# Two more second products in seven blocks instead of eight, with the weight work that feeds them moved

## The chip, the cores and the metric

The kernel runs on 1 core of a Trainium2 chip. The metric is device time in microseconds (us) of one execution, the median of several; lower is better. One core has TensorE (PE, matrix products), VectorE (DVE), ScalarE (ACT), GpSimd (POOL) and SyncE (SP, here the queue of nearly all DMAs).

## The reference

Linear attention with an RMS norm, then a dense network with SiLU, then four experts with ReLU, whose outputs are added under normalised weights. All inputs are float32.

```
kv = einsum('bhsd,bhse->bhde', k, v); out = einsum('bhsd,bhde->bhse', q, kv)
x = out / sqrt(mean(out*out, -1) + 1e-6) * g_norm        # -> 2304 tokens x 512
h = x @ w_in; x = (h * sigmoid(h)) @ w_out               # 512 -> 2048 -> 512
p = probs / (probs.sum(-1) + 1e-9)
out = sum over e of p[:, e] * (relu(x @ w1[e]) @ w2[e])   # 4 experts, 512 -> 1024 -> 512
```

## The kernel before, in words

The tokens are cut in three groups of 768 (NP = 3). The dense network is cut in four experts of 512 hidden units (groups 0 to 3), the four real experts in eight halves of 512 (groups 4 to 11). A *step* n works one expert on one token group: steps -12 to -1 are the dense network (group g has steps 3g-12 to 3g-10), steps 0 to 23 the experts. So steps -6 to -4 are group 2, steps -3 to -1 group 3, steps 0 to 2 group 4.

A step has two matrix products, 512x512 by 512x768. A float32 operand is kept as a high part (ACT, `hi`) and a remainder (DVE or POOL, `lo`), and three part products are added. A product is done either in eight blocks of 12 matmuls (`second`, "plain") or by a scheme with seven block products and extra sums (`again`, "seven blocks"). The seven need the weights' four quarters' sums s1 to s4 (`fsum`, `sumw`, DVE), sums t1 to t4 of the hidden values (`sumh`, DVE), their splits (`hhi` on ACT, `hlo` on DVE, for t3 and t4 on POOL), and seven additions into the accumulator (`gather`, DVE) where plain needs four. The first product (`first`) has seven blocks in every step from -9 on. Which steps have a second product of seven blocks, the function `seven` says (L138): in before -9, -8, -7, -5, -4, -3 and all from 1 on.

TensorE's order is written by hand. Time is counted in *slots*; a block of 12 matmuls is one slot. `start[n]` is the slot at which step n begins, and a first block of step n alternates with a second block of step n-1. A step's stretch is 7 slots plus 7 or 8 for the second product of the step before it. Every other operation is put at a slot (`put(slot, f, ...)`); events are sorted by slot and recorded in that order, so the tables of slots (SUM_AT, SPLIT_AT, W1_AT, W2_AT, CONVERT) fix each engine's queue. Each engine works its queue in order and waits where an operand or a buffer isn't ready. A table's slots count from the start of the group's first step.

The names used later: L467 `gather` (acc<-ps_ox, ps_oz or ps_o), L414 `add` (f<-ps_z), L454 `sumh` (f<-f), L152 `lo` (hid, w, x), L149 `hi`, L234 `fsum`, L292 `sumw`, L196, L197 and L201 the conversion of one dense weight chunk on VectorE (`cv3` is two instructions, `cv4` one), L207 its end on POOL, L326 `xsum`, L273 and L280 the loads of an expert's first and second weights, L347 and L359 the stores and loads of split tokens. PSUM holds two banks for the second products; a bank can be written again when its `gather` has read it. Buffers: five `w2`, two `w2b` (s3, s4), seven `w1`, eight `raw`. `swap` (slot -23.6) gives the memory of the dense weights to the `raw` loads.

## Time and profile before

| what | us |
|---|---|
| three timed runs | 1147.37, 1146.85, 1147.36 (median 1147.36) |
| the profiled execution, its own time | 1146.34 |
| its span, first to last instruction | 1144.6 |
| TensorE busy | 1134.5 (99%) |
| VectorE busy | 950.2 (83%) |
| ScalarE busy | 515.7 (45%) |
| GpSimd busy | 335.1 (29%) |

The 1.7 us between span and time lie around the program. Matmuls are pipelined, so one of 12 shows 0.34 us though a block takes 2.09. All the rows quoted are of this one execution.

### The profile page before, as it was taken

The numbers are of one execution on the slowest core, as the hardware profiler recorded it, in microseconds if no ns is written. First come the engines' busy times: TensorE is split into PE (matmuls) and PEld (weight loads), VectorE is DVE, ScalarE is ACT, GpSimd is POOL, SyncE is SP. The second block draws the span as 40 slices with busy tenths as digits, with TensorE's granted clock in tenths as the row PEclk, the third lists the DMA queues.
The fourth block names the chain that finished last, engine by engine and source line by source line (L and its number), as shares of the span: only waits on it lengthen the run. The fifth ranks groups of instructions, "written<-read, shape, count | busy, mean of one in ns | idle before, by whom it ended". The sixth has DMA issues, their size and how long they took to land.

```text
span 1144.6 us, 17104 instructions
## 1 busy us (share of the span) xinstructions
PE 1134.5 (99%) x6673; PEld 1128.5 (99%) x6673; DVE 950.2 (83%) x1080; ACT 515.7 (45%) x730; POOL 335.1 (29%) x198
## 2 busy tenths in 40 slices
PE   9999999999999999999999999999999999999998
PEld 8999999999999999999999999999999999999998
DVE  3997768987987587699799899899889889889874
ACT  4885565555554454544333333333333333333334
POOL 4943213331221344132232222232232232223211
PEclk9999999999999999999999999999999999999999
DMA  9967876666656662695675776675686685686604
GB/s 365 361 241 259 296 294 245 219 208 222 229 191 212 196 235 100 249 311 196 237 240 205 234 253 203 217 253 202 216 268 208 204 271 198 205 278 207 207 32 162
DMA packets 70035, 261.23 MB, mean 228 GB/s; under 512 B 7804, under 2 KB 26180, under 8 KB 69444
## 3 DMA queue, kind: packets, MB, share of 16 engines
q1 hardware_dynamic: 69668, 260.11, 65.2%
q8 instruction: 53, 0.87, 0.3%
q14 instruction: 26, 0.21, 0.1%
q10 hardware_dynamic: 288, 0.04, 0.0%
HBM read 222.34 MB, written 37.79 MB: 227 GB/s over the span
## 4 chain that ended last, share of the span: by engine, by line
PE 88%; DVE 6%; DMA 2%; ACT 2%; issue 1%; POOL 0%; SPq 0%; DVEq 0%; ACTq 0%; POOLq 0%
PE ps_x L369 22%; PE ps_ox L369 19%; PE ps_z L369 16%; PE ps_oz L369 15%; PE ps_o L498 9%; PE ps_h L397 4%; DMA kv_raw<-in_kv 2%; DVE hid L152 1%; ACT hid L149 1%; PE p_o L858 1%; PE ps_kv L836 1%; DVE acc L467 1%; DVE f L454 1%; DVE f L414 1%; ACT f L424 1%; DMA wd_raw<-in_wd 1%
## 5 line engine op out<-in xcount | busy, mean ns | idle before, releaser
L149 ACT ACTIVATE hid<-f 128x768 fp32r<-128x768 f32 x231 | 192.1, 843 | 370.4 <-DVE f L454 195.4
L152 POOL TENSOR_TENSOR hid<-f,hid 128x768 fp32r<-128x768 f32 x82 | 162.9, 1987 | 569.9 <-ACT hid L149 438.4
L369 PE MATMUL ps_x<-x,w 128*128 128x384 f32 x1584 | 297.0, 335 | 0.0
L369 PEld LDWEIGHTS ps_x<-x,w 128*128 128x128 f32 x1584 | 277.7, 188 | 0.0
L369 PE MATMUL ps_ox<-hid,w 128*128 128x384 f32 x1392 | 261.4, 335 | 0.6 <-DVE acc L467 0.6
L369 PEld LDWEIGHTS ps_ox<-hid,w 128*128 128x128 f32 x1392 | 243.2, 188 | 1.0 <-ACT hid L149 0.9
L369 PE MATMUL ps_z<-x,w 128*128 128x384 f32 x1188 | 222.8, 335 | 0.0
L369 PEld LDWEIGHTS ps_z<-x,w 128*128 128x128 f32 x1188 | 208.3, 188 | 0.0
L369 PE MATMUL ps_oz<-hid,w 128*128 128x384 f32 x1044 | 196.4, 335 | 1.8 <-DVE acc L467 1.3
L152 DVE TENSOR_TENSOR hid<-f,hid 128x768 fp32r<-128x768 f32 x149 | 153.0, 1028 | 52.3 <-ACT hid L149 52.2
L369 PEld LDWEIGHTS ps_oz<-hid,w 128*128 128x128 f32 x1044 | 182.3, 188 | 3.0 <-DVE acc L467 2.0
L498 PE MATMUL ps_o<-hid,w 128*128 128x384 f32 x672 | 124.2, 334 | 0.0
L454 DVE TENSOR_TENSOR f<-f 128x768 f32<-128x768 f32 x116 | 115.2, 993 | 2.7 <-ACT f L424 1.2
L498 PEld LDWEIGHTS ps_o<-hid,w 128*128 128x128 f32 x672 | 117.3, 188 | 0.0
L467 DVE TENSOR_TENSOR acc<-ps_ox,acc 128x768 f32<-128x768 f32 x109 | 103.6, 951 | 14.1 <-PE ps_ox L369 13.2
L414 DVE TENSOR_TENSOR f<-ps_z,f 128x768 f32<-128x768 f32 x66 | 62.9, 953 | 39.8 <-PE ps_z L369 39.8
L449 DVE SCALAR_TENSOR_TENSOR f<-f,pb 128x768 f32<-128x768 f32 x72 | 86.6, 1203 | 2.5
L467 DVE TENSOR_TENSOR acc<-ps_oz,acc 128x768 f32<-128x768 f32 x85 | 80.8, 951 | 8.9 <-PE ps_oz L369 8.1
L149 ACT ACTIVATE w<-s 128x512 fp32r<-128x512 f32 x88 | 54.9, 624 | 54.9 <-DVE s L292 29.2
L207 POOL TENSOR_TENSOR full<-full,wd_raw 128x512 int32<-128x512 int32 x32 | 47.9, 1497 | 103.8 <-DVE full L201 60.9
L409 ACT ACTIVATE f<-ps_x 128x768 f32<-128x768 f32 x66 | 53.3, 807 | 35.1 <-PE ps_x L369 35.0
L152 DVE TENSOR_TENSOR w<-s,w 128x512 fp32r<-128x512 f32 x74 | 53.3, 727 | 5.4 <-ACT w L149 4.7
(77 smaller groups left out, 955.8 us busy)
## 6 DMA issues: line engine op xcount, KB each, us to landing
x<-x_dram SPq DMA_DIRECT2D x210, 768.0 KB, 4.3
x_dram<-x SPq DMA_DIRECT2D x42, 768.0 KB, 5.2
wd_raw<-in_wd SPq DMA_DIRECT2D x32, 512.0 KB, 4.7
raw<-in_w SPq DMA_DIRECT2D x128, 128.0 KB, 4.6
kv_raw<-in_kv SPq DMA_DIRECT2D x18, 512.0 KB, 10.3
pb<-p_dram SPq DMA_DIRECT2D x24, 384.0 KB, 5.0
q_raw<-in_qt SPq DMA_DIRECT2D x4, 1152.0 KB, 11.6
out<-o SPq DMA_DIRECT2D x6, 512.0 KB, 2.8
```

Source lines behind the costliest of these rows:

```text
L149: self.nc.scalar.activation(t[:, 0], f, AF.Copy)
L152: (eng or self.nc.vector).tensor_tensor(t[:, 1], f, t[:, 0].bitcast(F32), op=ALU.subtract)
L207: self.nc.gpsimd.tensor_tensor(f, f, self.words(c, i, 0, I32), op=ALU.add)
L369: self.nc.tensor.matmul(p[:, f, :HN], w[0][:, a, c : c + 128], x[:, b, kp, :], start=self.FRESH[k] and a == b == kp == 0, stop=b == kp == ...
L397: self.nc.tensor.matmul(p, w[:, u, c : c + 128], self.x[n, f"b{k + 1}{j + 1}"][:, v, kp, :], start=u == v == k == kp == 0, stop=v == k == ...
L409: self.nc.scalar.activation(t, self.of_ps(n, c), AF.Copy)
L414: self.nc.vector.tensor_tensor(t, self.of_ps(n, c), t, op=ALU.add)
L424: self.nc.scalar.activation(self.f[n, name], src, AF.Silu)
L449: self.nc.vector.scalar_tensor_tensor(f, src, 0.0, self.probs(n, int(name[2]) - 1), op0=ALU.max, op1=ALU.mult)
L454: self.nc.vector.tensor_tensor(f, self.f[n, a], self.f[n, b], op=ALU.subtract)
L467: self.nc.vector.tensor_tensor(a, self.of_ps(n, k), a, op=ALU.add)
L498: self.nc.tensor.matmul(self.ps[n, b][:, e, :HN], w[:, u, c : c + 128], h[:, v, kp, :], start=self.count[key] == 1, stop=self.count[key] = ...
```

## The change

Steps -6 and 0 become steps of seven blocks. Their s weights (group 2 and group 4) must then be ready for their first step, so tables of slots change: the first weights of the dense groups (`SUM1_AT`, `SPLIT1_AT`, now tables for each group), the second weights of group 2 (`SUM_AT[2]`, `SPLIT_AT[2]`), the conversions (`CONVERT`), and group 4's loads, sums and splits (the first entries of `W1_AT`, `W2_AT`). Six splits of group 4's weights and two of the tokens (b21 of steps 1 and 2) go from GpSimd to VectorE. The later places of c11, c21 and t4, which steps 0 to 22 had, now hold for the dense steps too. Each of the groups 2 and 4 splits one quarter fewer, a21.

```
-        return n >= 1 or n in (-9, -8, -7, -5, -4, -3)
+        return n >= 0 or n in (-9, -8, -7, -6, -5, -4, -3)
...
-        2: dict(a11=2.4, a12=4.4, a21=6.4, a22=14.5, s1=15.9, s4=17.1, s3=18.3, s2=29.2),
+        2: dict(a11=6.5, s1=8, s2=8.6, s4=15.5, s3=19.2, a12=20.4, a22=21.5),
...
-    CONVERT = {1: (6.5, 9, 18.5, 20.5, 22.5, 25.5, 31, 35), 2: (6, 8.5, 15, 19.2, 20.8, 22.4, 24, 31.8)}
+    CONVERT = {1: (13, 16, 18.2, 22.4, 24, 27, 30.4, 32.4), 2: (13, 16, 18.2, 22.4, 24, 27, 30.4, 32.4)}
...
-                    for name, at in (("s1", -6.6), ("s2", -6.5), ("s3", -1.6), ("s4", -1.5)):
+                    split = dict(zip(self.A, self.SPLIT1_AT[e]))
+                    sums = dict(zip(("s1", "s2", "s4", "s3"), self.SUM1_AT[e]))
+                    for name, at in sums.items():
                         put(b0 + at, self.fsum, e, 0, name)
...
-        late = 0 <= n < self.steps - 1
+        late = n < self.steps - 1
...
-        load=(-8, -4), s1=(5.5, 7.2), s2=(5.6, 7.5), s4=(9.4, 9.4), s3=(11, 9.6),
+        load=(-23.5, -4), s1=(-19, 7.2), s2=(-18.9, 7.5), s4=(-18.2, 9.4), s3=(-16.2, 9.6),
...
-        on_pool = (self.A if i == 0 else ("a12", "s3", "a22")), (("a11", "a21", "a22") if i == 0 else ())
+        on_pool = ("a12", "s3", "a22"), ()
...
-                    put(b0 + at[k] + 0.01, self.xlo, n, name, pool if k in ((0, 1, 5) if n else (1, 3, 5)) else None)
+                    put(b0 + at[k] + 0.01, self.xlo, n, name, pool if k in ((0, 5) if n else (1, 3, 5)) else None)
```

VectorE's queue in the stretch where step -7's second product alternates with step -6's first (228 to 260 us in the trace), from one `gather` of bank oz to the next; before:

```order
L467 TENSOR_TENSOR acc<-ps_oz,acc 128x2x384
L152 TENSOR_TENSOR hid<-f,hid 128x768
L414 TENSOR_TENSOR f<-ps_z,f 128x768
L454 TENSOR_TENSOR f<-f 128x768
L152 TENSOR_TENSOR w_2438<-full_1960,w_2438 128x512
L467 TENSOR_TENSOR acc<-ps_ox,acc 128x2x384
L152 TENSOR_TENSOR hid<-f,hid 128x768
L196 TENSOR_SCALAR full_2475<-full_2475 128x512
L197 TENSOR_SCALAR full_2475<-full_2475 128x512
L201 SCALAR_TENSOR_TENSOR full_2475<-wd_raw,full_2475 128x512
L152 TENSOR_TENSOR w_2480<-full_1960,w_2480 128x512
L467 TENSOR_TENSOR acc<-ps_oz,acc 128x2x384
```

and with the change (the lines from L234 on stand six further down there):

```order
L473 TENSOR_TENSOR acc<-ps_oz,acc 128x2x384
L420 TENSOR_TENSOR f<-ps_z,f 128x768
L473 TENSOR_TENSOR acc<-ps_ox,acc 128x2x384
L152 TENSOR_TENSOR hid<-f,hid 128x768
L460 TENSOR_TENSOR f<-f 128x768
L152 TENSOR_TENSOR hid<-f,hid 128x768
L152 TENSOR_TENSOR w_2455<-s,w_2455 128x512
L152 TENSOR_TENSOR w_2463<-full_1976,w_2463 128x512
L473 TENSOR_TENSOR acc<-ps_oz,acc 128x2x384
```

The conversion (L196 to L201) is gone from here, and the bank's ox `gather` stands third instead of sixth.

VectorE's queue some 15 slots later, where step -6's second product runs, from an `add` to the next `gather` but one; before:

```order
L414 TENSOR_TENSOR f<-ps_z,f 128x768
L152 TENSOR_TENSOR w_2708<-s,w_2708 128x512
L152 TENSOR_TENSOR hid<-f,hid 128x768
L196 TENSOR_SCALAR full_2475<-full_2475 128x512
L197 TENSOR_SCALAR full_2475<-full_2475 128x512
L201 SCALAR_TENSOR_TENSOR full_2475<-wd_raw,full_2475 128x512
L467 TENSOR_TENSOR acc<-ps_o,acc 128x2x384
```

and with the change:

```order
L420 TENSOR_TENSOR f<-ps_z,f 128x768
L196 TENSOR_SCALAR full_2598<-full_2598 128x512
L197 TENSOR_SCALAR full_2598<-full_2598 128x512
L201 SCALAR_TENSOR_TENSOR full_2598<-wd_raw,full_2598 128x512
L473 TENSOR_TENSOR acc<-ps_ox,acc 128x2x384
L152 TENSOR_TENSOR hid<-f,hid 128x768
L460 TENSOR_TENSOR f<-f 128x768
L152 TENSOR_TENSOR w_2724<-s,w_2724 128x512
L152 TENSOR_TENSOR hid<-f,hid 128x768
L152 TENSOR_TENSOR w_2748<-full_1976,w_2748 128x512
L473 TENSOR_TENSOR acc<-ps_oz,acc 128x2x384
```

Two gathers stand where one stood, with a `sumh` and two more weight splits between.

SP's queue at the first loads of group 4's weights (raw1 first weights, raw2 second, x2 the split tokens that a later step reads); before:

```order
L359 DMA x2_3517<-x_dram_73 128x1536
L273 DMA raw1_3550<-in_w 128x256 x2
L273 DMA raw1_3567<-in_w 128x256 x2
L359 DMA x2_3570<-x_dram_73 128x1536
L273 DMA raw1_3572<-in_w 128x256 x2
L273 DMA raw1_3588<-in_w 128x256 x2
L359 DMA x2_3605<-x_dram_73 128x1536
```

and with the change:

```order
L365 DMA x2_3512<-x_dram_73 128x1536
L286 DMA raw2_3545<-in_w 128x256 x2
L286 DMA raw2_3561<-in_w 128x256 x2
L286 DMA raw2_3568<-in_w 128x256 x2
L365 DMA x2_3572<-x_dram_73 128x1536
L286 DMA raw2_3586<-in_w 128x256 x2
L279 DMA raw1_3590<-in_w 128x256 x2
L279 DMA raw1_3607<-in_w 128x256 x2
L365 DMA x2_3610<-x_dram_73 128x1536
L279 DMA raw1_3612<-in_w 128x256 x2
L279 DMA raw1_3628<-in_w 128x256 x2
```

The second weights' eight DMAs, which stood among the token stores after them, now come first.

## Rows read from the trace of the kernel before

**Rows 1.** The page's head: the span, then busy time, share and instructions.

```profile
span 1144.6 us, 17104 instructions
PE 1134.5 (99%) x6673; PEld 1128.5 (99%) x6673; DVE 950.2 (83%) x1080; ACT 515.7 (45%) x730; POOL 335.1 (29%) x198
```

**Rows 2.** TensorE's timeline, 227 to 297 us: start, us, block [idle, releaser].

```profile
228.23 2.25 PE L369 MATMUL ps_ox<-hid,w 128*128 128x384 f32 x12
...
251.71 2.40 PE L369 MATMUL ps_oz<-hid,w 128*128 128x384 f32 x12 [0.98 <-DVE acc L467]
...
260.20 2.25 PE L498 MATMUL ps_o<-hid,w 128*128 128x384 f32 x12
...
291.50 2.24 PE L369 MATMUL ps_ox<-hid,w 128*128 128x384 f32 x12
...
296.28 0.41 PE L369 MATMUL ps_oz<-hid,w 128*128 128x384 f32 x1 [0.45 <-ACT hid L149]
```

**Rows 3.** Stretch by stretch, one a step: length, each engine's busy time, clock, DMA.

```profile
199.01:228.23 29.22, 29.22 (x170) 29.22 (x169) 26.96 (x31) 15.60 (x22) 9.31 (x5) 1.00 0.62 214
228.23:260.20 31.97, 30.09 (x169) 29.16 (x169) 27.35 (x31) 16.98 (x25) 10.51 (x6) 1.00 0.65 223
260.20:291.50 31.30, 31.30 (x182) 31.30 (x182) 23.57 (x33) 16.09 (x25) 6.88 (x5) 1.00 0.67 235
291.50:321.43 29.93, 29.48 (x170) 29.19 (x170) 27.38 (x31) 14.91 (x22) 7.20 (x4) 1.00 0.59 205
...
442.44:473.73 31.29, 31.29 (x181) 31.29 (x181) 22.09 (x22) 14.97 (x20) 11.58 (x6) 1.00 0.59 223
473.73:503.09 29.36, 29.36 (x169) 29.18 (x169) 24.12 (x27) 14.60 (x20) 8.45 (x5) 1.00 0.76 262
```

**Rows 4.** VectorE's timeline: start, us, instruction [idle before it, releaser].

```profile
230.39 2.04 DVE L454 TENSOR_TENSOR f<-f 128x768 f32<-128x768 f32 x1
...
250.70 0.95 DVE L467 TENSOR_TENSOR acc<-ps_oz,acc 128x768 f32<-128x768 f32 x1
...
371.77 0.96 DVE L414 TENSOR_TENSOR f<-ps_x,f 128x768 f32<-128x768 f32 x1 [1.20 <-PE ps_x L369]
```

**Rows 5.** VectorE by form: xcount | busy us, mean ns of one | idle before.

```profile
L152 DVE TENSOR_TENSOR hid<-f,hid 128x768 fp32r<-128x768 f32 x149 | 153.0, 1028 | 52.3 <-ACT hid L149 52.2
L454 DVE TENSOR_TENSOR f<-f 128x768 f32<-128x768 f32 x116 | 115.2, 993 | 2.7 <-ACT f L424 1.2
L467 DVE TENSOR_TENSOR acc<-ps_ox,acc 128x768 f32<-128x768 f32 x109 | 103.6, 951 | 14.1 <-PE ps_ox L369 13.2
...
L414 DVE TENSOR_TENSOR f<-ps_z,f 128x768 f32<-128x768 f32 x66 | 62.9, 953 | 39.8 <-PE ps_z L369 39.8
L152 DVE TENSOR_TENSOR w<-s,w 128x512 fp32r<-128x512 f32 x74 | 53.3, 727 | 5.4 <-ACT w L149 4.7
L152 DVE TENSOR_TENSOR w<-raw,w 128x512 fp32r<-128x512 f32 x29 | 37.1, 1281 | 0.0
L152 DVE TENSOR_TENSOR x<-acc,x 128x768 fp32r<-128x768 f32 x33 | 33.6, 1030 | 10.9 <-ACT x L149 10.9
...
L201 DVE SCALAR_TENSOR_TENSOR full<-wd_raw,full 128x512 int32<-128x512 int32 x32 | 22.0, 689 | 0.6
L196 DVE TENSOR_SCALAR full<-full 128x512 f32<-128x512 f32 x32 | 21.1, 661 | 12.0 <-ACT full L189 11.7
...
L197 DVE TENSOR_SCALAR full<-full 128x512 int32<-128x512 int32 x32 | 14.7, 458 | 1.1
...
L234 DVE TENSOR_TENSOR s<-full 128x512 f32<-128x512 f32 x12 | 10.6, 884 | 0.0
```

**Rows 6.** SP's issues of L273, 355 to 375 us, and how long they took to land.

```profile
359.58 6.04 SPq L273 DMA_DIRECT2D raw<-in_w  x4
...
DMA to landing us min/median/max: 2.2/4.8/6.0
```

**Rows 7.** GpSimd's timeline, 228 to 232 us.

```profile
230.08 1.53 POOL L152 TENSOR_TENSOR w<-s,w 128x512 fp32r<-128x512 f32 x1 [10.46 <-ACT w L149]
```

More of the change, by code (lines that the diff above doesn't have):

```diff
@@ L219 @@
     )
-    SUM_AT = {1: (5, 5.1, 6.5, 8), 2: (15.4, 15.5, 16.8, 18), 3: (7.6, 7.7, 12, 14)}
+    SUM1_AT = {1: (-7.6, -7.5, -2.6, -2.4), 2: (-7.6, -7.5, -5.1, -4.5), 3: (-7.6, -7.5, -5.1, -4.5)}
+    SPLIT1_AT = {
[3 rows of a table added]
+    }
+    SUM_AT = {1: (5, 5.1, 6.5, 8), 2: (7.2, 7.5, 9.4, 9.6), 3: (7.6, 7.7, 12, 14)}
     SPLIT_AT = {
         1: dict(a11=6, s4=7.2, s3=8.6, s1=10.8, s2=11.8, a12=14.8, a22=16),
-        2: dict(a11=2.4, a12=4.4, a21=6.4, a22=14.5, s1=15.9, s4=17.1, s3=18.3, s2=29.2),
+        2: dict(a11=6.5, s1=8, s2=8.6, s4=15.5, s3=19.2, a12=20.4, a22=21.5),
         3: dict(a11=6, s1=8.5, s2=10.5, s4=12.5, s3=14.5, a12=16, a22=18, a21=18.2),
     }
-    CONVERT = {1: (6.5, 9, 18.5, 20.5, 22.5, 25.5, 31, 35), 2: (6, 8.5, 15, 19.2, 20.8, 22.4, 24, 31.8)}
+    CONVERT = {1: (13, 16, 18.2, 22.4, 24, 27, 30.4, 32.4), 2: (13, 16, 18.2, 22.4, 24, 27, 30.4, 32.4)}
     def fsum(self, e, i, name):
@@ L579, in first_events @@
                 if e > 0:
-                    for name, at in (("s1", -6.6), ("s2", -6.5), ("s3", -1.6), ("s4", -1.5)):
+                    split = dict(zip(self.A, self.SPLIT1_AT[e]))
+                    sums = dict(zip(("s1", "s2", "s4", "s3"), self.SUM1_AT[e]))
+                    for name, at in sums.items():
                         put(b0 + at, self.fsum, e, 0, name)
-                    for k in range(7):
-                        put(b0 - 9 + 2 * k, self.fhi, e, 0, k)
-                        put(b0 - 8.6 + 2 * k, self.flo, e, 0, k, pool if k in (1, 4, 6) else None)
-                        if self.A[k][0] == "s":
-                            put(b0 + (-1.4 if k == 2 else -8.5 + 2 * k), self.done_sum, e, 0, self.A[k])
-                    put(b0 + 3.6, self.done_full, e, 0)
+                        end = max(split[name] + 0.4, *(sums[x] for x, of in self.SUMS.items() if name in of), -99)
+                        put(b0 + end + 0.05, self.done_sum, e, 0, name)
+                    for k, at in enumerate(split.values()):
+                        put(b0 + at, self.fhi, e, 0, k)
+                        put(b0 + at + 0.4, self.flo, e, 0, k, pool if k in (1, 4, 6) else None)
+                    put(b0 + max(*split.values(), *sums.values()) + 0.5, self.done_full, e, 0)
                     for at, name in zip(self.SUM_AT[e], ("s1", "s2", "s4", "s3")):
@@ L673 @@
     W1_AT = dict(
-        load=(-23.2, -13), s1=(-11, -7.6), s2=(-10.9, -7.5), s4=(-4.9, -5.1), s3=(-6.9, -4.5),
+        load=(-21.4, -13), s1=(-11, -7.6), s2=(-10.9, -7.5), s4=(-4.9, -5.1), s3=(-6.9, -4.5),
         op=((-13.2, -11.2, -9.2, -7.2, -5.2, -3.2, -1.2), (-7.9, -7.8, -6.8, -5.8, 0.5, 6, 6.8)),
@@ L677 @@
     W2_AT = dict(
-        load=(-8, -4), s1=(5.5, 7.2), s2=(5.6, 7.5), s4=(9.4, 9.4), s3=(11, 9.6),
+        load=(-23.5, -4), s1=(-19, 7.2), s2=(-18.9, 7.5), s4=(-18.2, 9.4), s3=(-16.2, 9.6),
         op=(
-            dict(s1=6.6, s4=10.4, s3=11.5, a11=7.2, a12=8.6, a21=15.2, a22=17.7, s2=29.4),
+            dict(s1=-18.4, s4=-16.6, s3=-15.6, a11=6.6, s2=9, a12=14.6, a22=17),
             dict(a11=6.5, s1=8, s2=8.6, s4=15.5, s3=19.2, a12=20.4, a22=21.5),
@@ L738, in events @@
             put(b0 + 12.2, self.ps.pop, (n, "z"))
-            for slot, name in ((4.3, "c11"), (10.3, "c22"), (12.25, "c12"), (14.05 if n else 13.1, "c21")):
+            for slot, name in ((4.3, "c11"), (10.3, "c22"), (12.25, "c12"), (14.05, "c21")):
                 put(b0 + slot, self.relu, n, name)
@@ L743, in events @@
             put(b0 + 14.07, self.pb.pop, n)
-            if self.seven(n):
-                self.seven_events(put, n)
-            else:
-                for slot, name in ((5.3 if n else 6.15, "c11"), (10.5, "c22"), (12.5, "c12"), (14.1, "c21")):
-                    put(b0 + slot, self.hhi, n, name)
-                    put(b0 + slot + 0.01, self.hlo, n, name, pool if name == "c22" else None)
-                self.plain_events(put, n)
+            self.seven_events(put, n)
         end = self.start[self.steps]
```

3 rows, old and new, of the table SPLIT1_AT are left out of this document.

## The prediction

> **What bounds the kernel now.** The page's head comes first: TensorE is busy 1134.5 of 1144.6 us [rows 1], so whatever shortens TensorE's own row of work shortens the kernel, and everything else counts only where it makes TensorE wait. TensorE's timeline is read next: between waits the blocks follow each other without a break. The fifteen blocks from 260.20 to 291.50 [rows 2] give 31.30 / 15 = 2.087 us a block, which is one slot. Then the stretches, one a step [rows 3]. An undisturbed one of fourteen blocks lasts 29.22 us (199.01 to 228.23). The next, also of fourteen, lasts 31.97: 2.75 us of waits, the last of them at 251.71 for an `acc` of VectorE [rows 2]; that `gather` started at 250.70 and took 0.95 [rows 4], and freed the bank too late. The stretch from 291.50 has fourteen blocks and lasts 29.93: 0.71 us, around 296.28 [rows 2, 3]. These two places, 3.46 us together, lie inside the change's reach. Stretches that VectorE fills to 26.96 of 29.22 us ran without a wait [rows 3]; I take that as the nearest row for what it can carry.
>
> **TensorE's part.** Seven block products instead of eight: 12 matmuls fewer in step -6 and 12 in step 0, two blocks, 2 x 2.087 = 4.17 us. They lie on the path itself, since neither stretch (260.20 to 291.50, 442.44 to 473.73) holds a wait [rows 3]. Nothing hides them, so this gain is sure unless something else comes late.
>
> **VectorE's part.** A converted step needs 3 gathers, 4 hidden sums and 1 split more on VectorE: 3 x 0.951 + 4 x 0.993 + 1.028 = 7.85 us [rows 5], twice. Six weight splits and two token splits come from GpSimd. All of that lies beside TensorE; it costs nothing as long as VectorE isn't late. So I count each stretch anew, from the order of the changed program and the mean durations of rows 5 (a conversion is L196 + L197 + L201 = 0.661 + 0.458 + 0.689 = 1.81; a weight sum 0.884; a weight split from `s` or `full` 0.727).
>
> Common to a stretch of seven blocks in the dense part: 7 gathers 6.66, 5 hidden splits 5.14, 4 hidden sums 3.97, 3 adds 2.86, together 18.63 us. To that come
>
> - the stretch of step -7's second product (before: 228.23 to 260.20): 4 weight splits, 4 weight sums, 1 conversion, 2.91 + 3.54 + 1.81 = 8.26, so 26.89 us in 29.2. Before it was 27.35 in 31.97. The conversions and a12, a21 no longer stand between the gathers there, the light part is the front, where the three waits were.
> - that of step -6's: 4 weight splits and 5 conversions, 2.91 + 9.04 = 11.95, so 30.58 us in 29.2, where before it was 23.57 in 31.30. It is over full by 1.38.
> - that of step -5's: 3 splits, 4 sums, 2 conversions, 2.18 + 3.54 + 3.62 = 9.34, so 27.97 in 29.2.
> - that of step 0's (before: 442.44 to 473.73): the measured 22.09 [rows 3], plus 4 gathers 3.80, 2 hidden splits 2.06, 2 hidden sums 1.99, 1 token split 1.03, 2 weight splits from `raw` 2.56, less one split 0.73 and one ReLU 0.95 (priced as a gather) that now fall outside: 31.85 in 29.2, over full by 2.65. The stretch after it holds 24.12 in 29.36 and has room to catch up.
>
> **Sum of the likeliest case.** The blocks give 4.17. The 2.75 of waits go: the bank's `gather` that ended them now has three instructions fewer ahead of it and no conversion. The 0.71 goes too: TensorE waited there for a bank that a plain step's last gather had just read, and with step -6 in seven blocks no plain step stands there. At 0 to 1 that border moves to -1 to 0, where the gather comes after a stretch of light VectorE work; I count nothing. Together 7.63. Against it stand new waits in the two over full stretches. Their bounds: nothing, if VectorE's lag is carried and worked off later, and 1.38 + 2.65 = 4.03, if all of it becomes waiting. I take 1.3, a third, because a bank is written again three slots (6.3 us) after its block ended, so a gather may start 5.3 us late before TensorE waits, and a lighter stretch follows each. So 7.63 - 1.3 = 6.3 us faster. The profiled execution took 1146.34, which is 1.02 under the median of 1147.36; I take the difference off the median: 1141.0 us.
>
> **Other edits, at nothing.** ScalarE gains three high parts a converted step beside 16 of 31 us of work [rows 3]. GpSimd has four hidden splits more and nine weight and token operations less; it's at 7 to 12 of 31 us. The loads of group 4's second weights now come first in SP's queue. The first four DMAs of that place were issued from 359.58 over 6.04 us, held by the memory of the dense weights, and land in 2.2 to 6.0 us [rows 6]. The sum that reads them stands at slot -19, 371.5 us in this trace (291.50 is slot -57; 38 slots and 0.71 us of waits later), and later sums wait for later tiles. VectorE idles just then, 1.20 us before 371.77 [rows 4], and its queue is short; a landing late by a microsecond or two is covered. Behind the sum are an `add` and gathers of steps -2 and -3, and behind these TensorE. The token loads that the eight DMAs pass are read some twelve slots later by the table of slots.
>
> GpSimd and VectorE: a hidden sum at 230.39 took 2.04 us against a mean of 0.993 while GpSimd ran a split from 230.08 for 1.53 [rows 4, 5, 7], so it ran when GpSimd had ended, some 1.05 us late. The Trainium skill (SBUF — State Buffer, section Who interferes with whom) says that a VectorE instruction with two SBUF inputs and a GpSimd one that reads SBUF lock each other out for the whole instruction; the trace agrees with the 1.05 us. It speaks against the four new hidden splits on GpSimd (up to 4 x 1.05 = 4.2 us of VectorE's time) and for the nine operations taken off it (up to 9.5). My sum holds the mean of such delays in its durations and nothing more.
>
> **Rivals.**
> 1. *Clean*: VectorE carries its lag everywhere and no new wait comes. For it: the stretch with 26.96 busy had none, and 27.38 was reached in 29.93 [rows 3]. Against it: 30.58 and 31.85 are above anything in the rows. 1147.36 - 7.63 = 1139.7 us.
> 2. *All of the excess waits*: the lag turns into waits where it arises, 4.03 us. 1147.36 - 7.63 + 4.03 = 1143.8 us.
> 3. *VectorE becomes the bound, slower than before*. Its own waits for ScalarE and TensorE can't be filled: in the full stretch 29.22 - 26.96 = 2.26 us stayed idle [rows 3]. With 2.26 in each, the stretches of -6, -5 and 0 need 32.84, 30.23 and 34.11 us, over by 3.62, 1.01 and 4.89, together 9.52. If the four new GpSimd splits each hold up an instruction by 1.05 as at 230.39, 4.2 more: 13.7. 1147.36 - 7.63 + 13.7 = 1153.4 us. It decides from 9.9 us of new waits on (7.63 + 2.3). Against it: before, the same idle time was there, and VectorE shows lag without any wait in most stretches. Without the 4.2 it ends at 1149.2, no change that can be measured.
> 4. *The three waits stay*, since they come from the burst at the end of the stretch before and not from the conversions. 1141.0 + 2.75 = 1143.8, as rival 2.
>
> **Chances and range.** What a measurement of this kernel can tell from no change is about 0.2%, 2.3 us. The likeliest case (1140 to 1142.5) has 0.50, clean 0.17, rivals 2 and 4 together 0.20, between there and no change 0.08, slower 0.05. So faster 0.87, within 0.2% 0.08, slower 0.05. The range from 1139.2 (clean, less half a microsecond of scatter as the three runs show) to 1144.2 (rivals 2 and 4 with the same scatter) leaves out the last two.
>
> **What would show it.** In the changed profile, the stretches of steps -6 and 0 have fourteen blocks and last 29.2 us plus waits; if both show 31.3 the first step is wrong. No wait for `acc` between step -7's first and last block, or rival 4 holds. VectorE busy near 30 us and TensorE's new waits, if any, in step -6's and step 0's stretches, and 1 to 2 us in all; over 4 us there makes the forecast wrong, over 9.9 us gives rival 3. At slot -19 VectorE shows no long wait for a `raw` load.

## The result, and the profile after

The changed kernel takes 1157.66 us (median of four, 1156.91 to 1158.9) against 1147.11 for the kernel before on the same chip: 1.0093 times as long, interval 1.0076 to 1.0111. The forecast was 1141.0, faster; it came out slower. The profiled span grew from 1144.6 to 1155.2 us, 10.6 us. The page's head, answering to [rows 1]:

```profile
span 1155.2 us, 17075 instructions
PE 1134.5 (98%) x6649; PEld 1127.4 (98%) x6649; DVE 970.3 (84%) x1103; ACT 518.4 (45%) x734; POOL 328.8 (28%) x193
```

TensorE has 24 matmuls fewer and is as long busy as before. So it ran slower somewhere and waited more. Where, the stretches say (the columns and the six stretches of [rows 3], in the same order):

```profile
199.03:234.22 35.19, 31.37 (x169) 30.73 (x169) 31.78 (x36) 15.39 (x23) 9.79 (x6) 0.95 0.52 198
234.22:263.43 29.21, 29.21 (x169) 29.21 (x169) 23.41 (x27) 14.43 (x20) 7.47 (x4) 1.00 0.67 226
263.43:294.51 31.08, 29.56 (x170) 29.15 (x169) 29.82 (x37) 18.16 (x27) 11.29 (x7) 1.00 0.58 213
294.51:331.08 36.57, 31.03 (x169) 30.41 (x169) 32.73 (x38) 17.50 (x26) 10.23 (x6) 0.95 0.54 208
...
452.10:482.61 30.51, 29.72 (x170) 29.14 (x169) 26.82 (x27) 15.16 (x20) 10.83 (x5) 1.00 0.59 213
482.61:513.75 31.14, 29.77 (x169) 29.13 (x169) 29.53 (x30) 15.11 (x21) 9.51 (x6) 1.00 0.76 255
```

| stretch of the second product of step | before | after | difference | what it is |
|---|---|---|---|---|
| -8 | 29.22 | 35.19 | +5.97 | new waits |
| -7 | 31.97 | 29.21 | -2.76 | the three old waits are gone |
| -6 | 31.30 | 31.08 | -0.22 | a block less (-2.09), a new wait (+1.86) |
| -5 | 29.93 | 36.57 | +6.64 | new waits (7.35), the old 0.71 gone |
| 0 | 31.29 | 30.51 | -0.78 | a block less (-2.09), new waits (+1.31) |
| 1 | 29.36 | 31.14 | +1.78 | new waits |
| sum | | | +10.63 | the whole difference of the spans |

Two stretches hold 13.3 us of it. TensorE's timeline (as [rows 2]) shows one block of bank oz in each, late for a `gather`, and a smaller wait for a weight split in step -6's:

```profile
224.17 3.42 PE L375 MATMUL ps_oz<-hid,w 128*128 128x384 f32 x12 [3.62 <-DVE acc L473]
227.39 2.81 PE L375 MATMUL ps_z<-x,w 128*128 128x384 f32 x12
...
281.98 2.21 PE L375 MATMUL ps_ox<-hid,w 128*128 128x384 f32 x11 [1.52 <-DVE w L152]
...
321.35 3.64 PE L375 MATMUL ps_oz<-hid,w 128*128 128x384 f32 x12 [5.15 <-DVE acc L473]
```

The block after the first wait took 227.39 - 224.17 = 3.22 us instead of 2.09. The same stretches cut at the wait show why (the value behind GpSimd's busy time is the granted clock):

```profile
220.55:224.17 3.62, 0.00 (x0) 0.00 (x0) 3.62 (x4) 1.85 (x3) 2.15 (x2) 1.00 0.60 212
224.17:227.39 3.22, 3.22 (x12) 3.22 (x13) 3.22 (x6) 0.00 (x0) 0.00 (x0) 0.66 0.01 6
227.39:230.05 2.66, 2.66 (x14) 2.66 (x13) 1.74 (x3) 1.69 (x2) 0.00 (x0) 0.77 0.00 0
230.05:232.20 2.15, 2.15 (x14) 2.15 (x14) 1.82 (x2) 0.30 (x1) 0.00 (x0) 1.00 0.44 77
...
321.35:324.82 3.47, 3.47 (x12) 3.47 (x13) 3.47 (x6) 0.00 (x0) 0.00 (x0) 0.59 0.00 0
```

After an idle time of 3.62 us the granted clock was 0.66 and then 0.77 of 2.4 GHz, part of the time at its lower level of 1.2 GHz; after 5.15 us it was 0.59. The slower blocks cost 1.13 + 0.57 and 1.38 us, 3.1 of the 13.3.

VectorE's queue up to that first late gather:

```profile
209.95 1.67 DVE L196 TENSOR_SCALAR full<-full 128x512 f32<-128x512 f32 x1 [0.60 <-ACT full L189]
211.66 1.42 DVE L197 TENSOR_SCALAR full<-full 128x512 int32<-128x512 int32 x1
...
218.66 0.68 DVE L240 TENSOR_TENSOR s<-full 128x512 f32<-128x512 f32 x1
219.38 2.19 DVE L240 TENSOR_TENSOR s<-s,full 128x512 f32<-128x512 f32 x1
221.50 1.75 DVE L152 TENSOR_TENSOR w<-full,w 128x512 fp32r<-128x512 f32 x1
223.18 0.94 DVE L473 TENSOR_TENSOR acc<-ps_oz,acc 128x768 f32<-128x768 f32 x1
```

and GpSimd's beside it:

```profile
218.84 2.19 POOL L152 TENSOR_TENSOR hid<-f,hid 128x768 fp32r<-128x768 f32 x1 [2.85 <-ACT hid L149]
220.99 1.71 POOL L152 TENSOR_TENSOR w<-full,w 128x512 fp32r<-128x512 f32 x1
```

VectorE is hardly idle from 210 to 223 us. It is simply late: a conversion, then the next group's two weight sums and the split a11, all ahead of the gather. Two of these end about half a microsecond after GpSimd's splits do (219.38 + 2.19 = 221.57 against 221.03; 221.50 + 1.75 = 223.25 against 222.70), which fits their running most of their 0.69 us only when those were over. The gather starts 223.18 - 199.03 = 24.15 us after its stretch began; before, the same one started 17.38 us after it.

### The profile page after: what moved, and what is told of

It reads as the page before. It is cut to its first block, busy times and chain, and to the rows that moved or that the text cites. A ratio compares the mean times of both kernels' runs of the same rounds, so it can differ in the third digit from the quotient of the medians.

```text
span 1155.2 us, 17075 instructions
## 1 busy us (share of the span) xinstructions
PE 1134.5 (98%) x6649; PEld 1127.4 (98%) x6649; DVE 970.3 (84%) x1103; ACT 518.4 (45%) x734; POOL 328.8 (28%) x193
## 4 chain that ended last, share of the span: by engine, by line
PE 83%; DVE 11%; DMA 2%; ACT 2%; issue 1%; POOL 0%; SPq 0%; DVEq 0%; POOLq 0%; ACTq 0%
PE ps_x L375 20%; PE ps_ox L375 19%; PE ps_z L375 15%; PE ps_oz L375 14%; PE ps_o L504 7%; PE ps_h L403 4%; DMA kv_raw<-in_kv 2%; DVE hid L152 2%; DVE acc L473 2%; DVE f L460 1%; PE p_o L860 1%; DVE w L152 1%; DVE full L201 1%; DVE full L196 1%; DVE f L420 1%
## 5 line engine op out<-in xcount | busy, mean ns | idle before, releaser
L149 ACT ACTIVATE hid<-f 128x768 fp32r<-128x768 f32 x237 | 197.2, 843 | 389.9 <-DVE f L460 215.5
L152 POOL TENSOR_TENSOR hid<-f,hid 128x768 fp32r<-128x768 f32 x86 | 170.4, 1981 | 558.4 <-ACT hid L149 410.7
L375 PE MATMUL ps_ox<-hid,w 128*128 128x384 f32 x1488 | 279.8, 335 | 3.1 <-DVE acc L473 1.5
L375 PEld LDWEIGHTS ps_ox<-hid,w 128*128 128x128 f32 x1488 | 259.9, 188 | 4.3 <-DVE w L152 1.8
L375 PE MATMUL ps_oz<-hid,w 128*128 128x384 f32 x1116 | 212.3, 338 | 9.8 <-DVE acc L473 9.8
L375 PEld LDWEIGHTS ps_oz<-hid,w 128*128 128x128 f32 x1116 | 196.8, 190 | 11.4 <-DVE acc L473 11.0
L460 DVE TENSOR_TENSOR f<-f 128x768 f32<-128x768 f32 x124 | 120.4, 971 | 2.4 <-ACT f L430 0.3
L473 DVE TENSOR_TENSOR acc<-ps_ox,acc 128x768 f32<-128x768 f32 x114 | 108.3, 950 | 16.1 <-PE ps_ox L375 15.1
L504 PE MATMUL ps_o<-hid,w 128*128 128x384 f32 x480 | 88.4, 334 | 0.0
L504 PEld LDWEIGHTS ps_o<-hid,w 128*128 128x128 f32 x480 | 83.8, 188 | 0.0
```

What stands on the lines that cost most here:

```text
L149: self.nc.scalar.activation(t[:, 0], f, AF.Copy)
L152: (eng or self.nc.vector).tensor_tensor(t[:, 1], f, t[:, 0].bitcast(F32), op=ALU.subtract)
L375: self.nc.tensor.matmul(p[:, f, :HN], w[0][:, a, c : c + 128], x[:, b, kp, :], start=self.FRESH[k] and a == b == kp == 0, stop=b == kp == ...
L460: self.nc.vector.tensor_tensor(f, self.f[n, a], self.f[n, b], op=ALU.subtract)
L473: self.nc.vector.tensor_tensor(a, self.of_ps(n, k), a, op=ALU.add)
L504: self.nc.tensor.matmul(self.ps[n, b][:, e, :HN], w[:, u, c : c + 128], h[:, v, kp, :], start=self.count[key] == 1, stop=self.count[key] = ...
```

## Experiments

Theories for the 13.3 us: A, the first weights' sums and the split now stand ahead of the gather; B, the conversions, moved to the end of their row, make VectorE late before that; C, `late` moves the split of c21 and the sum t4 to later slots, ahead of the gather. In the table: when the gather of bank oz, quarter (0,1), starts, counted from the first block of its stretch.

| run | time, us | step -8's gather | step -5's gather | longest wait for a dense step, us |
|---|---|---|---|---|
| before | 1147.1 | 17.38 | 17.37 | 1.0 |
| after | 1157.7 | 24.15 | 25.84 | 5.1 |
| e1_late_off | 1156.5 | 23.15 | 22.75 | 3.1 |
| e2_first_back | 1151.6 | 20.04 | 20.45 | 2.6 |
| e3_conv_tail | 1150.7 | 17.90 | 17.94 | 2.5 |
| e5_spread | 1151.4 | 17.89 | 21.99 | 1.9 |
| e7_off_pool | 1155.3 | 23.07 | 24.79 | 4.1 |
| e16_after_fill | 1151.8 | 22.45 | 24.31 | 4.3 |
| e18_dense_fill2 | 1143.9 | 17.89 | 21.41 | 1.1 |

The block that needs the bank stands 20.87 us after the stretch's start when nothing waits, and where it was late for the gather it started 1.00 us after the gather did. So in these rows it came late by the gather's start less 19.87 us, less what the stretch had already waited (24.15 - 0.48 - 19.87 = 3.80, measured 3.78; 22.45 - 19.87 = 2.58, measured 2.58). A gather that starts up to 19.9 us after its stretch began costs nothing, and each microsecond beyond it is one of waiting: before, 2.5 us were to spare.

**One cause at a time**

```
-        late = n < self.steps - 1
+        late = 0 <= n < self.steps - 1
```

> The changed kernel (1157.7 us), with one edit: in the dense steps the gathers c11 and c21 and the add t4 go back to their old slots (4.7, 3.3, 4.6 in place of 5.8, 4.7, 5.6). The 13.3 us of new waits stand in two stretches: 5.97 us in that of step -8's second product and 7.35 us in that of step -5's, each for the gather oz of block (0,1). Theory C (the later c21 and t4 now stand in front of that gather): most of the 13.3 goes, 1145 to 1148 us. Theory A (the first weights' two sums and the split a11, put ahead of that gather): they still stand there, at most 3 us go, 1154 to 1158. Theory B (the conversions moved to slots 27 to 32.4 make VectorE late): 1156 to 1158.

1156.5 us, 1.2 less. C falls as the main cause: the gathers come 1.0 and 3.1 us earlier, and the wait in step -6's stretch grows from 1.5 to 3.1 us.

```
-    SUM1_AT = {1: (-7.6, -7.5, -2.6, -2.4), 2: (-7.6, -7.5, -5.1, -4.5), 3: (-7.6, -7.5, -5.1, -4.5)}
+    SUM1_AT = {e: (-6.6, -6.5, -1.5, -1.6) for e in (1, 2, 3)}
...
+    SPLIT1_AT = {e: (-9, -7, -5, -3, -1, 1, 3) for e in (1, 2, 3)}
```

> The changed kernel, with one edit: the sums and splits of the dense experts' first weights go back to their old slots (sums at -6.6, -6.5, -1.5, -1.6, splits every second slot from -9), so that two sums and the split a11 stand behind the gather oz of block (0,1) and no longer in front of it. Theory A: each of these three instructions was held to about 2 us there (2.19, 2.17 and 1.75 us), some 4 to 5 us of VectorE's time a place; without them the gather comes in time, most of the 13.3 us go: 1144 to 1148 us. Theory B: the lag from the conversions (5 to 6 us before the cluster) stays, at most half goes: 1151 to 1156. Theory C: 1155 to 1158, as the hidden split of c21 and the add t4 still come late.

1151.64 us, 6.0 less: inside B's range, at its lower end, and 3.6 above A's. The two gathers come 4.1 and 5.4 us earlier, and the stretch of -8 is down to 29.68 us. But step -6's goes from 31.08 to 34.99 us.

```
-    CONVERT = {1: (13, 16, 18.2, 22.4, 24, 27, 30.4, 32.4), 2: (13, 16, 18.2, 22.4, 24, 27, 30.4, 32.4)}
+    CONVERT = {1: (13, 16, 18.2, 22.4, 24, 27, 43.5, 45.5), 2: (13, 16, 18.2, 22.4, 24, 27, 43.5, 45.5)}
```

> The changed kernel, with one edit: the last two of the eight conversions of a dense group go from slots 30.4 and 32.4, just ahead of the late gather, to 43.5 and 45.5, behind it. Theory B: VectorE comes to the cluster with a lag of 2.4 in place of 5 to 6 us, and the gather 3 us or more earlier; the waits of 3.6 and 5.2 us for it and their followers go: 1145 to 1149 us. Theory A: the cluster of two sums and a split alone makes the gather late; a third or less goes, 1153 to 1157. Theory C: as A.

1150.67 us, 7.0 less, A's cluster still in place: between B's range and A's. Both gathers are in time (17.9). So A and B are not rivals: VectorE's lateness is one sum, and taking out either part brings the gathers back to 20.5 us or less. Again the rest of the time went to step -6's stretch, where a weight split is late (the columns of [rows 3]; step -8's and step -6's of this kernel):

```profile
199.07:228.29 29.22, 29.22 (x170) 29.22 (x169) 25.71 (x30) 13.38 (x19) 6.86 (x4) 1.00 0.63 224
...
258.89:293.84 34.95, 31.66 (x169) 30.53 (x169) 33.59 (x42) 19.86 (x29) 11.27 (x7) 0.95 0.54 207
```

**Step 0 alone.** The dense side as before, step 0 in seven blocks, with group 4's tables and the token split of b21 as in the change:

```
-        return n >= 1 or n in (-9, -8, -7, -5, -4, -3)
+        return n >= 0 or n in (-9, -8, -7, -5, -4, -3)
...
-        load=(-8, -4), s1=(5.5, 7.2), s2=(5.6, 7.5), s4=(9.4, 9.4), s3=(11, 9.6),
+        load=(-23.5, -4), s1=(-19, 7.2), s2=(-18.9, 7.5), s4=(-18.2, 9.4), s3=(-16.2, 9.6),
...
-        on_pool = (self.A if i == 0 else ("a12", "s3", "a22")), (("a11", "a21", "a22") if i == 0 else ())
+        on_pool = ("a12", "s3", "a22"), ()
```

> The kernel before, with the change's second half alone: step 0 in seven blocks, with the second weights of group 4 made ready early and three of their and the tokens' splits on VectorE; the dense side is that of before. If the two halves are independent, the block's 2.09 us go and the waits that the changed kernel shows in the stretches of steps 0 and 1 come (1.31 and 1.78 more than before): 1147.1 - 2.09 + 1.31 + 1.78 = 1148.1 us, no change that can be measured. If those waits are a late effect of the dense side's order (all theories A to C leave that open), they are missing: 1145.0 us.

1147.95 us, 1.0 above before (ratio 0.9999 to 1.0018, so not told apart from it), as expected if the halves are independent. The waits are step 0's own: 30.55 and 31.08 us for the two stretches, as in the changed kernel. In them VectorE and GpSimd run:

```profile
448.85 2.12 DVE L152 TENSOR_TENSOR w<-raw,w 128x512 fp32r<-128x512 f32 x1
452.45 1.04 DVE L152 TENSOR_TENSOR x<-acc,x 128x768 fp32r<-128x768 f32 x1 [1.48 <-ACT x L149]
453.42 2.60 DVE L326 TENSOR_TENSOR acc<-acc 128x768 f32<-128x768 f32 x1
```

```profile
448.37 2.05 POOL L152 TENSOR_TENSOR x<-acc,x 128x768 fp32r<-128x768 f32 x1 [10.81 <-ACT x L149]
450.39 2.29 POOL L152 TENSOR_TENSOR hid<-f,hid 128x768 fp32r<-128x768 f32 x1
452.63 2.57 POOL L152 TENSOR_TENSOR x<-acc,x 128x768 fp32r<-128x768 f32 x1
```

**Too much work, or badly placed?** From the run with the tail moved:

```
-    CONVERT = {1: (13, 16, 18.2, 22.4, 24, 27, 43.5, 45.5), 2: (13, 16, 18.2, 22.4, 24, 27, 43.5, 45.5)}
+    CONVERT = {1: (13, 16, 18.2, 22.4, 24, 27, 43.5, 45.5), 2: (13, 16, 20.5, 25, 28.5, 31.5, 43.5, 45.5)}
```

> The run with the last two conversions moved (1150.7 us), with four more conversions of the second dense group moved: slots 18.2, 22.4, 24 and 27 become 20.5, 25, 28.5 and 31.5, so that two leave the stretch of step -6's second product for that of step -5's. That stretch takes 34.95 us with 33.59 of VectorE in it and holds the largest wait left (2.49 us for a weight split, then slower blocks). Theory D (VectorE's work in that stretch is what is too much): two conversions of 1.81 us less, the stretch falls to 29.2 to 31 us, the run to 1145 to 1147 us. Theory E (the split a12 stands only 1.2 slots ahead of the block that reads it, so any lag of over 2 us makes TensorE wait there): the wait stays in part, 1148 to 1150 us. If the work only makes step -5's stretch late: 1150 or more.

1151.42 us, no gain: neither D's range nor E's, but the third outcome. The wait isn't gone but spread over three stretches, 32.10, 31.46 and 30.73 us:

```profile
259.27:291.37 32.10, 30.32 (x169) 29.03 (x169) 29.15 (x38) 17.96 (x27) 9.59 (x6) 1.00 0.55 197
291.37:322.83 31.46, 29.51 (x169) 29.19 (x169) 28.58 (x33) 15.67 (x23) 9.02 (x6) 1.00 0.71 251
322.83:353.56 30.73, 29.51 (x169) 29.19 (x169) 27.27 (x32) 15.56 (x24) 10.21 (x6) 1.00 0.53 180
```

Again from the run with the tail moved, its conversions not spread:

```
-        2: dict(a11=6.5, s1=8, s2=8.6, s4=15.5, s3=19.2, a12=20.4, a22=21.5),
+        2: dict(a11=6.5, s1=8, s2=8.6, s4=15.5, a12=18, s3=19.2, a22=20),
```

> The run with the last two conversions moved (1150.7 us), with the splits a12 and a22 of the second dense group's second weights put earlier: 20.4 to 18 and 21.5 to 20. Theory E (a12's place, 1.2 slots ahead of its use, is the cause of the 2.49 us wait): the wait and the slower blocks behind it go, up to 5.7 us, 1145 to 1147 us. Theory D (VectorE is too full in that stretch, its lag at 5 to 8 us): the wait moves to the gather or to the split that is now behind, 1149 to 1151 us.

1151.54 us, 0.9 more than without, 0.5 above D's range and far from E's. TensorE now waits 2.47 us for the next split instead: one put earlier only makes what stands behind it late, as D has it.

```
-        on_pool = {name: self.nc.gpsimd for name in (("t3", "t4") if n < 0 else ("c22", "t3", "t4"))}
+        on_pool = {name: self.nc.gpsimd for name in (("t3",) if n in (-8, -5) else ("t3", "t4") if n < 0 else ("c22", "t3", "t4"))}
...
-                        put(b0 + at + 0.4, self.flo, e, 0, k, pool if k in (1, 4, 6) else None)
+                        put(b0 + at + 0.4, self.flo, e, 0, k, pool if k in (4, 6) else None)
```

> The changed kernel (1157.7 us), with two splits taken from GpSimd to VectorE in the clusters ahead of the late gathers: the first weights' a12 (three times) and the hidden t4 of steps -8 and -5. The two sums and the split a11 there took 2.19, 2.17 and 1.75 us beside these two GpSimd splits, against 0.69 each where GpSimd stands still. If GpSimd's splits hold them up: 4.0 us of hold-ups go and 0.69 + 0.96 us of work come, the gather is 2.4 us earlier a place, and the two waits of 3.6 and 5.2 us shrink by as much, with the slower blocks behind them: 1150 to 1154 us. If the long durations have another cause (a wait inside the instruction for a tile), the gather is 1.65 us later a place: 1159 to 1162 us.

1155.3 us, 2.4 less: two instructions more for VectorE ahead of each gather, and yet the gathers come 1.1 us earlier. GpSimd does hold VectorE up, but the gain is half of the 2.4 us a place that were expected, and the time lies above the range: ahead of step -8's gather 2.58 us of long durations went and two instructions, 1.63 us, came.

From the run of step 0 alone:

```
-        on_pool = {name: self.nc.gpsimd for name in (("t3", "t4") if n < 0 else ("c22", "t3", "t4"))}
+        on_pool = {name: self.nc.gpsimd for name in (("t3", "t4") if n < 0 else () if n == 0 else ("c22", "t3", "t4"))}
```

> The run with step 0 alone in seven blocks (1147.95 us), with the hidden splits of c22, t3 and t4 of step 0 on VectorE instead of GpSimd. In it GpSimd's token split, t3 and second token split run back to back from 448.4 to 455.2 us while VectorE's a22 takes 2.12, the token sum 2.60 and a token split waits 1.48 us; VectorE then lags 5 to 7 us and TensorE waits 1.31 us more in step 0's stretch and 1.78 us more in step 1's. If GpSimd's hold-ups make that lag: three splits of 0.96 us more work against up to 4 us of hold-ups, the waits go at least by half, 1145 to 1146.5 us. If it is the sheer work (31.85 us in 29.2): 2.9 us more of it, 1149 to 1151 us.

1147.77 us, 0.2 less: step 0's stretch 30.17 us instead of 30.55, step 1's unchanged. That lies in neither range, decides nothing between the two, and is of no use.

From the changed kernel, the conversions alone:

```
-    CONVERT = {1: (13, 16, 18.2, 22.4, 24, 27, 30.4, 32.4), 2: (13, 16, 18.2, 22.4, 24, 27, 30.4, 32.4)}
+    CONVERT = {1: (8, 10.5, 13, 16, 18.2, 20.5, 23, 26), 2: (8.5, 11, 13.5, 17, 24, 28, 43.5, 45.5)}
```

> The changed kernel (1157.7 us), with the slots of the sixteen conversions alone changed: the first group's eight all before slot -100, in stretches where VectorE is light (15.65 of 29.8 us busy from 140.0 to 169.8 us), and the second group's two per stretch, so that the stretches of steps -9 to -4 hold 6, 0, 2, 3, 1 and 2 conversions where the changed kernel had 5, 3, 0, 6, 2 and 0. By the busy times of the run with the last two moved, VectorE then has some 27.5, 23.9, 25.8, 28.5, 27.7 and 26.2 us in 29.2. Theory F (waits come where a single stretch is given more than about 28 us of VectorE's work; no stretch has that now, and the seven blocks of step -6 can be carried): the dense side's waits fall from 8 us to 2 to 3, 1144.5 to 1147 us. Theory G (six stretches together are too full, and the waits only move, as in the runs tried so far, which all gave 1150.7 to 1151.6): 1149.5 to 1152 us.

1152.21 us: G, 0.2 above its range. My busy times were off too, 31.98 us for step -6's stretch instead of 28.5, and step -9's has a wait of its own now:

```profile
170.90:202.09 31.19, 29.50 (x169) 29.18 (x169) 27.82 (x37) 17.14 (x26) 12.45 (x8) 1.00 0.70 256
261.66:296.35 34.69, 30.56 (x169) 28.96 (x169) 31.98 (x39) 18.01 (x27) 8.94 (x6) 1.00 0.68 240
```

The same with step 0 plain, and its tables as before:

```
-        return n >= 0 or n in (-9, -8, -7, -6, -5, -4, -3)
+        return n >= 1 or n in (-9, -8, -7, -6, -5, -4, -3)
```

> The run with balanced conversions, with step 0 plain as before (its weights and splits too): the dense half of the change alone. The run of step 0 alone was 1.0 us above before (1147.95 against 1146.93), so this is 0.9 to 1.0 us below the balanced run: 1143.5 to 1146 us if theory F holds, 1148.5 to 1151 if G.

1150.93 us, 1.3 less than with step 0: theory G's range again.

The balanced run again, with step 0's three hidden splits on VectorE as above, and group 5's first sums and splits later:

```
-                put(b0 + at[name][i], self.sumw, e, part, name)
+                put(b0 + at[name][i] + (0.8 if e == E1 + 1 and part == 1 and name in ("s1", "s2") else 0), self.sumw, e, part, name)
...
-        ops = dict(zip(self.A, self.W1_AT["op"][i])), self.W2_AT["op"][i]
+        ops = dict(zip(self.A, self.W1_AT["op"][2 if e == E1 + 1 else i])), self.W2_AT["op"][i]
```

> The run with balanced conversions, with two edits behind step -1: step 0's three GpSimd hidden splits (c22, t3, t4) on VectorE, and in the fifth expert's first weights the two sums and the split a11 put behind the gather of block (0,1) instead of ahead of it. The first was worth 0.2 us alone (1147.77 against 1147.95). In step 1's stretch 1.7 us of waits are left, 1.1 of them for that gather, behind that same cluster of sums, split and GpSimd splits which made the dense side late. If the cluster is the cause, most of 1.7 us goes: 1.0 to 1.9 us below the balanced run. If the lag comes from step 0's extra work alone: within 0.4 us of it.

1151.65 us, 0.6 less, between the two ranges. The gather behind the cluster no longer waits (1.17 us gone), and the next one does, by 1.39 instead of 0.54: the cluster is where the lag shows; that it does not arise there too is not shown, as two edits were made at once.

**VectorE's own idle time.** Five placements had ended at 1150.7 to 1152.2 us. What they share is this, at the start of every stretch (VectorE, run with the tail moved):

```profile
222.22 0.96 DVE L473 TENSOR_TENSOR acc<-ps_oz,acc 128x768 f32<-128x768 f32 x1
224.08 0.96 DVE L152 TENSOR_TENSOR hid<-f,hid 128x768 fp32r<-128x768 f32 x1 [0.90 <-ACT hid L149]
...
227.27 0.95 DVE L460 TENSOR_TENSOR f<-f 128x768 f32<-128x768 f32 x1
229.14 0.96 DVE L152 TENSOR_TENSOR hid<-f,hid 128x768 fp32r<-128x768 f32 x1 [0.91 <-ACT hid L149]
```

VectorE adds, ScalarE makes a SiLU or a high part of it, and the next but one or the very next instruction in VectorE's queue needs that: 0.9 us idle, twice a stretch, full or not. So the two hidden splits go one or two instructions back:

```
             lo = at + (0.5 if at < b0 + 12 or late and name == "c21" else 0.005)
+            if n <= 2 and name in ("c22", "t1"):
+                lo = b0 + (12.15 if name == "c22" else 12.5015)
```

> The run with the conversions spread (1151.4 us), with two hidden splits of each seven-block step up to step 2 moved back in VectorE's queue by one or two instructions: c22's behind the add of c12, t1's behind the sum t2. In each stretch VectorE stands still 0.93 and 0.91 us ahead of these two, since ScalarE's SiLU and high part (0.85 us each) come between; behind them something else runs meanwhile. Theory H (the waits come since VectorE's work plus its own idle time passes 29.2 us a stretch: 28.6 + 2.6 where a wait of 2.24 us stood): 1.8 us a stretch are given back, the dense side's 8.0 us of waits in four stretches and step 0's and 1's 3 us fall by 4 to 8 us: 1143.5 to 1147.5 us. Theory I (single instructions held by GpSimd, or their place ahead of a gather, make the waits): within 1.5 us, 1150 to 1152 us.

> The same two splits moved back, in the run with only the last two conversions moved (1150.7 us). There the stretch of step -6 holds 33.6 us of VectorE and 5.7 us of waits, the others little. Theory H: that stretch stays over full (33.6 less hold-ups), so 2 to 4 us less: 1146.5 to 1149. Theory I: 1149.5 to 1151.5.

> The same two splits moved back, in the kernel before (1147.0 us). Its waits in the reach of the edit are 2.75 us in step -7's stretch and 0.71 us at 296.28 us. Theory H: the first go at least by half, 1144.5 to 1146 us. Theory I: 1146.5 to 1147.5.

> The same two splits moved back, in the kernel with step 0 alone in seven blocks (1147.95 us; c22 of steps 0 to 2 is GpSimd's and only comes later there). Its waits in reach: those of before and 1.31 + 1.78 us in the stretches of steps 0 and 1. Theory H: half of the sum of 6.5 us or more goes, 1142.5 to 1145 us, a kernel that beats both. Theory I: 1147 to 1148.5 us.

1146.87, 1144.55, 1144.83 and 1145.39 us. In the order given, each against the same kernel without the edit: -4.6, -6.1, -2.1 and -2.6 us. H holds on the dense side (the second even passed its range); for step 0 half of 6.5 us was expected and 2.6 came, 0.4 us short of the range and mostly from the dense waits. The first two runs scatter (1145.32 to 1147.99 and 1144.17 to 1146.04), so their gains are good to some 1.5 us. The queue of the second at that place:

```profile
222.49 0.96 DVE L473 TENSOR_TENSOR acc<-ps_oz,acc 128x768 f32<-128x768 f32 x1
224.65 0.96 DVE L420 TENSOR_TENSOR f<-ps_z,f 128x768 f32<-128x768 f32 x1 [1.20 <-PE ps_z L375]
225.53 0.95 DVE L152 TENSOR_TENSOR hid<-f,hid 128x768 fp32r<-128x768 f32 x1
226.67 0.96 DVE L473 TENSOR_TENSOR acc<-ps_ox,acc 128x768 f32<-128x768 f32 x1 [0.19 <-PE ps_ox L375]
227.54 1.94 DVE L460 TENSOR_TENSOR f<-f 128x768 f32<-128x768 f32 x2
229.40 0.96 DVE L152 TENSOR_TENSOR hid<-f,hid 128x768 fp32r<-128x768 f32 x1
```

VectorE waits for TensorE's newest block here now, not for ScalarE: it has caught up. Step -6's stretch fell from 34.95 to 31.64 us:

```profile
258.01:289.65 31.64, 29.54 (x170) 29.11 (x170) 31.26 (x40) 19.21 (x29) 11.28 (x7) 1.00 0.56 211
```

The same edit in the changed kernel itself:

> The changed kernel as it was timed (1157.7 us), with nothing but the two hidden splits of each seven-block step moved back in VectorE's queue (c22's behind the add of c12, t1's behind the sum t2). The conversions and the first weights stand where the change put them, and with them the cluster ahead of the late gathers. Theory H (a full stretch plus VectorE's own idle time): 0.9 + 0.9 us come back a stretch, the gathers that made TensorE wait 3.6 and 5.2 us come 1.8 us or more earlier, and the lag that enters the stretch is smaller too; half or more of the 13.3 us goes, 1147 to 1151 us. If the place of the conversions and the cluster alone decide: 1155 to 1157 us.

1151.84 us, 5.8 less, nothing else moved: step -8's stretch 31.90, step -6's 29.38, but step -5's still 36.06 us, with a gather at 24.31. A little over the range's upper end; idle time is a part of the cause, beside conversions and order.

The run with the tail and the two splits moved, step 0 plain as before:

```
-        return n >= 0 or n in (-9, -8, -7, -6, -5, -4, -3)
+        return n >= 1 or n in (-9, -8, -7, -6, -5, -4, -3)
```

> The dense half of the change with the last two conversions moved and the two splits moved back, step 0 plain as before. Step 0 in seven blocks cost 0.6 us where the splits were moved (1145.39 against 1144.83), so this is 0.5 to 0.6 us under the run with both (1144.55): 1143.5 to 1144.3 us. Against the kernel before with the same splits moved (1144.83) it shows what the block less is worth once VectorE's idle time is used: 0.5 to 1.3 us of 2.09, the rest being the 2.4 us wait in step -6's stretch less the 1.16 us one that stays in that kernel's step -7's.

1145.32 us, runs from 1144.17 to 1145.96: 1.0 to 1.8 above what I expected. The one wait left, 2.1 us for a weight split in step -6's stretch, was followed by slower blocks in the profiled run (33.16 us) and not in the run with step 0 (31.64). The two kernels' runs overlap from end to end (1144.17 to 1146.04 there), so the 0.8 us between their medians can't be put down to step 0. With the time goes the granted clock: 0.999 in the three runs up to 1144.45, 0.997 or 0.998 in the eight from 1145.1 on.

And from that run:

```
-    CONVERT = {1: (13, 16, 18.2, 22.4, 24, 27, 43.5, 45.5), 2: (13, 16, 18.2, 22.4, 24, 27, 43.5, 45.5)}
+    CONVERT = {1: (13, 16, 18.2, 22.4, 24, 27, 43.5, 45.5), 2: (13, 16, 22.2, 24.2, 26.2, 28.2, 43.5, 45.5)}
```

> The same with the second group's third to sixth conversions at slots 22.2, 24.2, 26.2 and 28.2 in place of 18.2, 22.4, 24 and 27: behind the weight splits a12 and a22 of that stretch, for which TensorE waits 2.1 us there. If the conversion ahead of a12 is what makes it late, the wait goes and no new one comes: 1141.5 to 1143 us. If VectorE's lag is only handed on to step -5's gather (as where they were spread, 2.57 us): 1143.5 to 1146 us.

1143.88 us (1143.12 to 1144.02), ratio to before 0.9972, interval 0.9961 to 0.9982: the fastest, and it beats both kernels. The wait for the split went, and step -5's gather came late by 1.1 us instead: the second outcome, but smaller than where they were spread.

```profile
258.49:287.97 29.48, 29.48 (x169) 29.12 (x169) 28.35 (x37) 18.21 (x29) 9.40 (x6) 1.00 0.60 217
287.97:318.86 30.89, 29.78 (x170) 29.16 (x169) 29.35 (x34) 14.76 (x21) 8.18 (x5) 1.00 0.72 254
```

Against the kernel before with the two splits moved (1144.83) the dense half is worth 0.95 of its 2.09 us (the kernel before took 1146.89 and 1147.02 beside the two).

## Why the prediction was wrong, point by point

- *Two blocks gone, 4.17 us on the path*: right. The stretches of steps -6 and 0 have fourteen blocks.
- *The 2.75 and the 0.71 us of old waits go*: right in number, and rival 4 is out, but the reasons are not shown. Step -7's stretch lost 2.76 us right after TensorE had stood still for some 4 us in step -8's, which left VectorE time to catch up. In the seven runs of the changed dense side without that pause (e2, e3, e5, e6, e9, e10, e11; those with the two splits moved left out) step -7's stretch lasted 30.1 to 30.6 us. In all but e2 conversions had come into it, so this doesn't settle it, but part of the 2.75 may be luck. For the 0.71 a plain step's last gather was named; the row names ScalarE's high part (they ended at 296.13 and 296.15), and with the two splits moved (e14) it went while step -6 was still plain, so VectorE's lateness had a part in it.
- *New waits 1.3 us, in the two stretches that were over full*: this step failed; 18.3 us came. In those two stretches it was 1.86 and 1.31 us, 3.2 together, inside the bound of 4.03. But 15.1 us more came in three stretches that I had held safe or not looked at: -4.17 - 3.46 + 1.86 + 1.31 + 5.97 + 7.35 + 1.78 = 10.64 us, the table's sum but for rounding.
- The stretch of step -8 was *never counted*, since no block of it changed. By the prediction's own method it has 18.63 + 3 conversions 5.43 + 4 sums 3.54 + 3 splits 2.18 = 29.78 us. Step -5's stretch was counted at 27.97; one conversion that stands just ahead of it by the slots runs inside it, as VectorE is late, which makes 29.78 too.
- Step 0's stretch was counted one gather too high: its three gathers were priced as four, and the one of bank o (444.75 us) stands in the measured 22.09 already; each quarter's first sum is ScalarE's copy there. Of the 31.85 us only 26.82 ran inside the stretch, the rest after its end.
- The limit was taken as 29.2. [Rows 3] had a warning: the fullest stretch without a wait there, 26.96 of 29.22 (later in that trace six of the experts' stretches have 27.49 of 29.21, from 591.03 on). The 2.26 us of idle time, which I put into rival 3 alone, stays in the dense steps' order. The runs that gave 1.8 us of it back won 2.1 to 6.1 us, and in e16 step -6's stretch held 29.04 us of VectorE in 29.38, nearly without a wait. Nor is 26.96 a safe limit: with 25.84 (e3, step -7's) TensorE waited 1.4 us.
- The allowance was right and misapplied: a gather may come some 5 us late (its block ended 14.6 us after the stretch began, and 19.87 was the latest start without a wait; before it started at 17.38). What counts is what stands ahead of one gather, not the stretch's sum. After a full stretch VectorE hands its lag on, as from step 0 to step 1, whose own work the change did not add to and which got 1.78 us: a sum that before started 4.0 us ahead of its stretch (469.73) now started 1.2 us into it (483.78).
- *GpSimd's splits in the means*: too low at these places, where instructions of 0.69 us took 2.19 and 1.75. Against the shortest of their kind, VectorE's instructions ahead of the gather took 5.6 us longer in step -8's stretch (before 2.5) and 5.1 in step -5's (before 1.7): 3.2 and 3.4 us of the 6.8 and 8.5 by which the gathers came later. Taking two splits off gave 2.4 us of the time.
- *The loads at nothing*: right. The sum that reads them started at 380.15, directly behind a gather, with no wait for a load.
- Rival 3 had the mechanism, the idle time and the hold-ups, at 1153.4 us and a chance of 0.05. Its places did not come out (3.62, 1.01 and 4.89 us for steps -6, -5 and 0, against 1.86, 7.35 and 1.31), and its price lacked step -8's stretch, step 1's, and 3.1 us of slower blocks.

Left open: how the 13.3 us divide between conversions, cluster, idle time and GpSimd, whose single effects overlap; and step 0, which still cost 0.56 us with the splits moved (1145.39 against 1144.83).
